# Forward DFT-47 as 24x24 products on sixteen 32x32 parts, with near and far frequencies formed on GpSimd

## The chip, the cores and the metric

The kernel runs on one core of a Trainium2 chip. The metric is the device time of one execution in microseconds (us). An execution is one launch over all inputs; the times below are those of whole executions, and the profile is that of one of them. Engines are named as in the profile: PE is TensorE's matmul, PEld its weight load, DVE is VectorE, ACT ScalarE, POOL GpSimd, and SP issues DMAs.

## What is computed

The reference is a Fourier layer along the sequence and an expert layer behind it (8 batches, 3008 positions, 256 channels, 2048 hidden units):

```python
X = np.fft.rfft(x, axis=1)
Yr = Xr @ w_r - Xi @ w_i + b_r
Yi = Xr @ w_i + Xi @ w_r + b_i
Yr = np.sign(Yr) * np.maximum(np.abs(Yr) - 0.01, 0.0)   # Yi alike
y = np.fft.irfft(Yr + 1j * Yi, n=3008, axis=1)
h = y.reshape(24064, 256) @ moe_w_in
out = (h * np.cos(h)) @ moe_w_out
```

## The kernel before

3008 is 64 x 47, two coprime lengths, so the transform of a batch is a DFT of length 64 and one of length 47 with an index order that needs no twiddle factors. The mixing matrices and the soft threshold (`wmix`) lie between the forward and the inverse transform. Each batch's Fourier work goes in these stages, by generator functions inside `tile_body`:

- `stage_a` (tiles `pa`, `ao`) does the forward DFT-64 and writes `scr1` in DRAM.
- `stage_b.load`, `forward` and `combine` do the forward DFT-47 for a quarter `q` of the 32 slots (eight slots). `load` brings the rows of `scr1` into `at`, and the constant `fq`. `forward` is one burst of 16 matmuls of 48x64 (`pb<-at,fq`): two groups `g` of 48 input rows (24 each of two symmetry parts or of real and imaginary part), an output block of 64 that holds the two halves `z` of 32, near and far frequency. Four banks `pb` receive it. DVE transposes each bank by 32x32 blocks into `at` again, and two DMAs by way of DRAM (`scrF`) turn it into `z`, where channels lie on partitions.
- `combine` (L598) makes of `z` the three operands of the mixing by matrices in split precision: real part, imaginary part and their sum `both`, each as a rounded value `Xh` (ACT) and a remainder `Xl`. POOL adds `both` (L610) and takes the remainders of `both` and of the imaginary part (`rest_pool`, L331), DVE those of the real part (`rest`, L334).
- `wmix` (tiles `pw`, L676 to L678) multiplies and thresholds; its `fold` (POOL, L706 to L718) turns signs by the table `sgn` and makes sums and differences for the inverse; `spread` does the inverse DFT-47 on sixteen 24x32 parts (`pi<-y,iw`) and writes `scr2`; `stage_c` (`pc`) does the inverse DFT-64 and gives `xTh`, `xTl`.

`moe_step` and `second` are the expert layer: for each of six tiles of up to 512 positions of a batch and each of 16 blocks `f` of hidden units six matmuls `ph` (L936 to L938), five elementwise passes on ACT and DVE with a cast `gh` and a remainder `gl`, and three steps later six matmuls `po` (L918 to L922). The remainder `gl` is taken by POOL for even `f` (L331) and by DVE for odd `f` (L334). Such a pair of `ph` and `po` groups is called a step here; there are 768.

Batch 0's Fourier work stands by itself ahead of everything and uses other code (`f2t1`). That of batch b + 1 is mixed into the expert steps of batch b: each generator yields a cost, and `pull` takes pieces as long as a budget lasts that each step adds to. The sum of these costs is written out by hand in `COST`; dividing it by the steps sets how densely the pieces are pulled. The instruction order of each engine then comes out of a scheduler that reorders within what is free to move, held by `floor()`, which ties a piece to the products of the second last step. A burst's matmuls are kept together:

```python
ins = mm(*calls[0][0], **calls[0][1])          # L373
...
with tc.high_priority(), tc.issue_after(ins.ins):
    for a, k in calls[1:]:
        ins = mm(*a, **k)                      # L383
```

So the first matmul of every burst has line L373 and the others have L383. In the trace a float32 matmul has two records, one for each of its two passes.

Of the kernel before, what the change touches and what calls it, by code (L numbers as in the profile page):

```python
# [88 lines left out]
def _constants():  # L89
# [17 lines left out]
    f1 = f1.transpose(0, 1, 3, 4, 2).reshape(128, 128)  # L107
    ei = ei.reshape(128, 128)
    fa = np.concatenate([fa.reshape(64, 64)] * 2)
# [4 lines left out]
    order = np.concatenate([np.arange(24), np.arange(46, 23, -1), [47]])  # L114
    f2 = np.zeros((32, 2, 48, 2, 48))
# [54 lines left out]
    c_fq = fq.transpose(1, 2, 0, 3, 4).reshape(128, 32 * 64).astype(np.float32)  # L170
    c_sig = np.concatenate([np.ones((48, 32)), sig.T]).astype(np.float32)
# [4 lines left out]
    c_sgn = c_sgn.astype(np.uint16)  # L176
    return [np.ascontiguousarray(a) for a in (c_fq, c_sig, c_f3, c_ff, c_if, c_iw, c_sgn)]


@with_exitstack  # L180
def tile_body(ctx: ExitStack, tc, x, w_r, w_i, b_r, b_i, w_in, w_out,
              c_fq, c_sig, c_f3, c_ff, c_if, c_iw, c_sgn, out):
    nc = tc.nc
# [355 lines left out]
    def stage_b(b):  # L539
# [15 lines left out]
        def load(q):  # L555
            if b and q < 4:
                fq = wk.tile([128, 512], F32, tag="fq", name="fq", bufs=2)
                with tc.issue_after(mark["x0"].ins) if b == 1 else ExitStack():
                    loads = [nc.gpsimd.dma_start(fq, c_fq[:, 512 * q:512 * q + 512])]
                t = wk.tile([128, 2048], F32, tag="at", name="at", bufs=1)  # L560
                for h in range(4):
                    own = q == 0 and SLOT0[h] != SLOTS[h]
                    r0 = 64 * (h // 2) + 24 * (h % 2)
# [10 lines left out]
        def forward(q):  # L574

            t, fq, loads = at.pop(q)
            p = some("pb", 4)
            burst(4, [((p[2 * e + g][64 * v:64 * v + 64, 256 * j:256 * j + 256],
                        fq[64 * g:64 * g + 48, 64 * i:64 * i + 64], t[64 * g:64 * g + 48, 256 * i:256 * i + 256]),
                       dict(start=j == 0, stop=j == 1, skip_group_check=True))  # L580
                      for e in range(2) for j in range(2) for v in range(2) for g in range(2) for i in (4 * v + 2 * e + j,)], loads)
            turned = t.rearrange("p (a g c e s k) -> p e g s c a k", a=4, g=2, c=2, e=2, s=2)
            for e in range(2):
                for g in range(2):
                    pv = p[2 * e + g]
                    drained(pv, nc.vector.transpose(turned[:, e, g], pv.rearrange("p (s c a k) -> p s c a k", s=2, c=2, a=4)))
                    if e == 0 or g == 0:
                        yield Hold(READ)
            f = dr.tile([128, 2048], F32, tag="scrF", name=f"scrF_{b}_{q}")
# [8 lines left out]
        def combine(q):  # L598

            z = Z.pop(q).rearrange("p (v z g m k) -> p g v z m k", v=2, z=2, g=2, m=8)[..., :24]  # L600
            xyh = wk.tile([128, 2304], F32R, tag="Xh", name="Xh", bufs=1)
            xyl = wk.tile([128, 2304], F32R, tag="Xl", name="Xl", bufs=1)
            hi, lo = ([m[:, 768 * r:768 * r + 768].rearrange("p (v m z k) -> p v z m k", v=2, m=8, z=2) for r in range(3)]
                      for m in (xyh, xyl))
            X[q] = tuple([[m[:, 768 * r:768 * r + 768].rearrange("p (v c x) -> p c v x", v=2, c=2)[:, c] for c in range(2)]
                          for r in range(3)] for m in (xyh, xyl))
            both = wk.tile([128, 1024], F32, tag="wx", name="both", bufs=3)[:, :768].rearrange("p (v m z k) -> p v z m k", v=2, m=8, z=2)
            for v in range(2):
                with floor():
                    nc.gpsimd.tensor_tensor(out=both[:, v], in0=z[:, 0, v], in1=z[:, 1, v], op=ALU.add)  # L610
                yield 0.9
                with floor():
                    nc.scalar.copy(hi[2][:, v], both[:, v])  # L613
                yield 0.8
            for v in range(2):
                with floor():
                    rest_pool(lo[2][:, v], both[:, v], hi[2][:, v])
                    nc.scalar.copy(hi[0][:, v], z[:, 0, v])
                yield 0.9
                with floor():  # L620
                    rest(lo[0][:, v], z[:, 0, v], hi[0][:, v])
                yield 0.9
            for v in range(2):
                with floor():
                    nc.scalar.copy(hi[1][:, v], z[:, 1, v])
                yield 0.8
                with floor():
                    rest_pool(lo[1][:, v], z[:, 1, v], hi[1][:, v])
                yield 1.2
# [70 lines left out]
        def fold(q, e):  # L700
# [14 lines left out]
            for r in range(2):  # L715
                po.tensor_tensor(out=od[:, 1 - r, first:, :23], in0=st[:, e, first:, r, 1:24],  # L716
                                 in1=st[:, e, first:, r, 24:47], op=ALU.subtract)
            po.tensor_tensor(out=st[:, e, first:, :, 1:24], in0=st[:, e, first:, :, 1:24],  # L718
                             in1=st[:, e, first:, :, 24:47], op=ALU.add)
            yield TURN  # L720
# [410 lines left out]
```

## Time and profile before

| | |
|---|---|
| median of 3 runs | 2578.68 us (2576.16 to 2579.6) |
| the profiled execution, its own time | 2579.13 us |
| span of the profile, first to last instruction | 2577.1 us |
| TensorE clock granted, mean | 0.998 |
| HBM traffic over the span | 109 GB/s |

The span is 2.0 us shorter than the execution's own time, which has the start and the end around it. A share is busy time over the span. In the timeline a row gives start and length, in us, of instructions of one line merged in order of time, their count, and in brackets idle time of the engine before it with what ended it. Busy time of PE is that of overlapping matmuls, so a stretch of it is measured from the start of one matmul to the start of a later one.

### The profile page before, as it was taken

To read this page: it belongs to the slowest core of one execution; us is meant where nothing else is said; L and a number is where in the kernel's file an instruction comes from. 1 tells how busy PE (TensorE), PEld (TensorE's weight loads), DVE (VectorE), ACT (ScalarE), POOL (GpSimd) and SP (SyncE) were. 2 spreads that over 40 slices of the span, in tenths; PEclk is the share of its full clock that TensorE was granted. 3 is DMA by queue.
4 is the path that set the end of the run, shared out by engine and by line. 5 is a ranking of instruction groups with operands and counts; after the bars stand their busy time and mean duration, and the time that the engine had idled before them with its cause. 6 is when DMAs were issued, how large, how long until landed. Compare 5 with 4: busy or idle time off the path is not lost.

```text
span 2577.1 us, 42991 instructions
## 1 busy us (share of the span) xinstructions
PE 2549.1 (99%) x15961; PEld 2063.7 (80%) x15961; DVE 1850.8 (72%) x2909; ACT 1679.6 (65%) x3119; POOL 1026.6 (40%) x1002
## 2 busy tenths in 40 slices
PE   9999999999999999999999999999999999999999
PEld 7577777877788777887788777887788888888888
DVE  5887766777667776777767777677776777766665
ACT  5766666666666666666666666666676666666666
POOL 2135552555334453345623545245442444222222
PEclk9999999999999999999999999999999999999999
DMA  7545444444334443254423544345433244210000
GB/s 238 188 115 148 134 116 118 112 130 139 111 82 126 136 132 98 82 154 142 130 83 98 155 131 119 91 101 144 132 104 104 85 116 114 62 45 17 17 25 16
DMA packets 172954, 283.12 MB, mean 110 GB/s; under 512 B 15608, under 2 KB 114200, under 8 KB 169160
## 3 DMA queue, kind: packets, MB, share of 16 engines
q1 hardware_dynamic: 161896, 243.78, 33.6%
q0 software_dynamic: 10112, 35.53, 4.4%
q8 instruction: 126, 2.06, 0.3%
q10 hardware_dynamic: 736, 1.05, 0.1%
q14 instruction: 84, 0.69, 0.1%
HBM read 149.76 MB, written 130.55 MB: 109 GB/s over the span
## 4 chain that ended last, share of the span: by engine, by line
PE 85%; DVE 5%; DMA 3%; ACT 2%; issue 2%; POOL 2%; SPq 0%; ACTq 0%; DVEq 0%; POOLq 0%
PE ph L936 12%; PE po L918 12%; PE po L922 12%; PE ph L937 12%; PE ph L938 12%; PE po L919 12%; PE pw L676 2%; PE pw L678 2%; PE pw L677 2%; PE pc L383 1%; PE pb L383 1%; DVE u L950 1%; DMA xt<-in_dram 1%; DVE u L947 1%; PE pw L672 1%
## 5 line engine op out<-in xcount | busy, mean ns | idle before, releaser
L331 POOL TENSOR_TENSOR gl<-u,gh 128x512 fp32r<-128x512 f32 (+1 forms) x384 | 494.0, 1286 | 1079.9 <-ACT gh L951 913.9
L949 ACT ACTIVATE u<-u 128x512 f32<-128x512 f32 (+1 forms) x768 | 478.4, 623 | 348.0 <-DVE u L947 346.9
L947 DVE SCALAR_TENSOR_TENSOR u<-ph,u 128x512 f32<-128x512 f32 (+1 forms) x768 | 515.9, 673 | 258.4 <-ACT u L946 256.5
L950 DVE TENSOR_TENSOR u<-ph,u 128x512 f32<-128x512 f32 (+1 forms) x768 | 518.5, 676 | 252.7 <-ACT u L949 240.5
L946 ACT ACTIVATE u<-ph 128x512 int32<-128x512 f32 (+1 forms) x768 | 449.9, 587 | 256.1 <-PE ph L938 248.0
L918 PE MATMUL po<-gh,wout 128*128 128x512 f32 (+1 forms) x1536 | 598.9, 390 | 4.4 <-ACT gh L951 4.4
L936 PE MATMUL ph<-xTh,win 128*128 128x512 f32 (+1 forms) x1536 | 601.5, 392 | 0.2
L951 ACT CAST gh<-u 128x512 fp32r<-128x512 f32 (+1 forms) x768 | 467.6, 610 | 202.3 <-DVE u L950 198.3
L937 PE MATMUL ph<-xTl,win 128*128 128x512 f32 (+1 forms) x1536 | 594.5, 387 | 0.0
L938 PE MATMUL ph<-xTh,win 128*128 128x512 f32 (+1 forms) x1536 | 594.0, 387 | 0.0
L919 PE MATMUL po<-gh,wout 128*128 128x512 f32 (+1 forms) x1536 | 593.6, 386 | 0.0
L922 PE MATMUL po<-gl,wout 128*128 128x512 f32 (+1 forms) x1536 | 477.8, 388 | 5.2 <-POOL gl L331 5.2
L334 DVE TENSOR_TENSOR gl<-u,gh 128x512 fp32r<-128x512 f32 (+1 forms) x384 | 304.6, 793 | 76.1 <-ACT gh L951 68.1
L936 PEld LDWEIGHTS ph<-xTh,win 128*128 128x128 f32 x1536 | 288.5, 188 | 87.5 <-issue 19.0
L922 PEld LDWEIGHTS po<-gl,wout 128*128 128x128 f32 x1536 | 287.2, 188 | 71.9 <-POOL gl L331 9.6
L918 PEld LDWEIGHTS po<-gh,wout 128*128 128x128 f32 x1536 | 288.6, 188 | 66.1 <-ACT gh L951 7.6
L938 PEld LDWEIGHTS ph<-xTh,win 128*128 128x128 f32 x1536 | 288.8, 188 | 56.3
L919 PEld LDWEIGHTS po<-gh,wout 128*128 128x128 f32 x1536 | 288.8, 188 | 51.1 <-issue 0.4
L937 PEld LDWEIGHTS ph<-xTl,win 128*128 128x128 f32 x1536 | 288.8, 188 | 51.0
L676 PE MATMUL pw<-Xh,wf 128*128 128x384 f32 x336 | 114.3, 340 | 2.9 <-ACT Xh L613 2.9
L716 POOL TENSOR_TENSOR odd<-st 128x184 f32<-128x184 f32 (+1 forms) x112 | 66.7, 595 | 122.0 <-DVE st L693 119.4
L677 PE MATMUL pw<-Xh,wf 128*128 128x384 f32 x336 | 113.4, 338 | 0.0
(119 smaller groups left out, 2443.6 us busy)
## 6 DMA issues: line engine op xcount, KB each, us to landing
scrF<-at SPq DMA_DIRECT2D x28, 1024.0 KB
z<-scrF SPq DMA_DIRECT2D x112, 256.0 KB
scrT<-tr SPq DMA_DIRECT2D x56, 512.0 KB
y<-scrT SPq DMA_DIRECT2D x112, 256.0 KB
bt<-scr SPq DMA_DIRECT2D x94, 256.0 KB
scr<-bo SPq DMA_DIRECT2D x224, 96.0 KB
scr<-ao SPq DMA_DIRECT2D x80, 256.0 KB
out_dram<-ob SPq DMA_DIRECT2D x80, 256.0 KB
```

Of the source, the lines that this page charges most:

```text
L331: return nc.gpsimd.tensor_tensor(out=lo, in0=x, in1=hi.bitcast(F32), op=ALU.subtract)
L918: mm(po[e][:, :n], wo[0][:, 0, f, es], gh[:, :n], start=f == 0, stop=False)
L919: mm(po[e][:, :n], wo[0][:, 1, f, es], gh[:, :n], start=False, stop=False)
L922: mm(po[e][:, :n], wo[0][:, 0, f, es], gl[:, :n], start=False, stop=f == NFC - 1)
L936: mm(h, win[:, 0, c, fs], th[:, c, :n], start=c == 0, stop=False)
L937: mm(h, win[:, 0, c, fs], tl[:, c, :n], start=False, stop=False)
L938: ins = mm(h, win[:, 1, c, fs], th[:, c, :n], start=False, stop=c == 1)
L946: nc.scalar.activation(k[:, :n], h, AF.Identity, bias=0.25, scale=1.0 / TWO_PI)
L947: nc.vector.scalar_tensor_tensor(out=u[:, :n], in0=h, scalar=1.0 / TWO_PI, in1=k[:, :n], op0=ALU.mult, op1=ALU.subtract)
L949: nc.scalar.activation(u[:, :n], u[:, :n], AF.Sin, bias=HALF_PI, scale=TWO_PI)
L950: product = nc.vector.tensor_tensor(out=u[:, :n], in0=h, in1=u[:, :n], op=ALU.mult)
L951: step = [nc.scalar.copy(gh[:, :n], u[:, :n])]
```

## The change

The forward burst of batches 1 to 7 is cut into 32 matmuls of 24x32 in place of 16 of 48x64: one for each of four row groups `h` of 24 input rows (at partitions 0, 32, 64 and 96), and each of the eight slots. A row group no longer adds over the two symmetry parts inside the matmul, and near and far frequency are no longer two outputs; instead `z` holds the two parts apart. `combine` makes near as their sum and far as their difference, for the real part (`re`) and the imaginary part (`im`), and multiplies the far half of `im` by a table `far` of signs: five more POOL instructions per quarter. Real and imaginary part then lie in whole runs, and everything behind works on halves of 384 elements that are contiguous. The order of the 48 output frequencies changes so that the empty one stands first in the far half; the fold reads 25 to 47 in place of 24 to 46. `fq` is half as large, slot 0 is kept in another form, and `COST` has 15.5 in place of 11.0 for the new yields.

```diff
-    fq = np.zeros((32, 2, 64, 2, 32))
+    fq = np.zeros((32, 2, 2, 32, 32))
...
-                fq[sl, g, 24 * o:24 * o + 24, :, :24] = parts[v, sl, r, :, g]
+                fq[sl, g, o, :24, :24] = parts[v, sl, r if sl else 0, :, g, 0]
...
+    far = sig[:, :24] * sig[:, 24:]
+    far[0] *= -1
...
+    turn_far = cp.tile([128, 32, 24], BF16, name="far")
...
+        nc.gpsimd.dma_start(turn_far.rearrange("p s k -> p (s k)"), c_far.bitcast(BF16))
...
             p = some("pb", 4)
-            burst(4, [((p[2 * e + g][64 * v:64 * v + 64, 256 * j:256 * j + 256],
-                        fq[64 * g:64 * g + 48, 64 * i:64 * i + 64], t[64 * g:64 * g + 48, 256 * i:256 * i + 256]),
-                       dict(start=j == 0, stop=j == 1, skip_group_check=True))
-                      for e in range(2) for j in range(2) for v in range(2) for g in range(2) for i in (4 * v + 2 * e + j,)], loads)
...
+            burst(4, [((p[h][64 * v + 32 * j:64 * v + 32 * j + 32, 256 * e:256 * e + 256],
+                        fq[32 * h:32 * h + 24, 32 * i:32 * i + 32], t[32 * h:32 * h + 24, 256 * i:256 * i + 256]),
+                       dict(start=e == 0, stop=e == 1, skip_group_check=True))
+                      for e in range(2) for v in range(2) for j in range(2) for h in range(4) for i in (4 * e + 2 * v + j,)], loads)
...
+            part = [wk.tile([128, 1024], F32, tag="wx", name=n, bufs=3)[:, :768] for n in ("re", "im", "both")]
+            both = part[2]
+            with_far = turn_far[:, 8 * q:8 * q + 8].unsqueeze(1).to_broadcast([128, 2, 8, 24])
+            for r in range(2):
+                for n, op in enumerate((ALU.add, ALU.subtract)):
+                    to = part[r].rearrange("p (m w z k) -> p z w m k", m=4, w=4, z=2)[:, n]
+                    with floor():
+                        nc.gpsimd.tensor_tensor(out=to, in0=z[:, 2 * r], in1=z[:, 2 * r + 1], op=op)
+                    yield 0.9
+            with floor():
+                far = part[1].rearrange("p (c y z k) -> p z c y k", c=2, y=8, z=2)[:, 1]
+                nc.gpsimd.tensor_tensor(out=far, in0=far, in1=with_far, op=ALU.mult)
+            yield 0.9
...
-                    nc.gpsimd.tensor_tensor(out=both[:, v], in0=z[:, 0, v], in1=z[:, 1, v], op=ALU.add)
+                    nc.gpsimd.tensor_tensor(out=cut(both, v), in0=cut(part[0], v), in1=cut(part[1], v), op=ALU.add)
...
-    COST = 4 * (6 * GROUP + 2 * TURN + 11.0 + MIXED + QUIET + 3 * READ + BURST + QUIET + 3 * READ + BURST)
+    COST = 4 * (6 * GROUP + 2 * TURN + 15.5 + MIXED + QUIET + 3 * READ + BURST + QUIET + 3 * READ + BURST)
```

The change also moves instructions on every engine, since the scheduler orders them anew. Two places are shown. The first is PE's order at the last quarter's forward burst of batch 3 (`po`, `ph`: expert layer; `pb`: the burst), before:

```order
L918 MATMUL po_8994<-gh,wout 128x512
L919 MATMUL po_8994<-gh,wout 128x512
L373 MATMUL pb<-at,fq 64x256
L383 MATMUL pb<-at,fq 64x256 x15
L936 MATMUL ph<-xTh,win 128x512
L937 MATMUL ph<-xTl,win 128x512
```

and now:

```order
L944 MATMUL po_9243<-gl,wout 128x512
L944 MATMUL po_9244<-gl,wout 128x512
L380 MATMUL pb<-at,fq 32x256
L390 MATMUL pb<-at,fq 32x256 x31
L958 MATMUL ph<-xTh,win 128x512
L959 MATMUL ph<-xTl,win 128x512
```

The burst stands at the same step, between whole groups of `po` and `ph`, and has twice as many matmuls with half as many output rows each. The second place is POOL's order at the combination of the last quarter of batch 3 (`gl`: expert layer; `st<-st`: the fold's sum), before:

```order
L331 TENSOR_TENSOR gl<-u,gh 128x512
L610 TENSOR_TENSOR both<-z 128x2x8x24 x2
L718 TENSOR_TENSOR st<-st 128x16x23
L331 TENSOR_TENSOR Xl<-both,Xh 128x2x8x24 x2
L331 TENSOR_TENSOR gl<-u,gh 128x512
L331 TENSOR_TENSOR Xl<-z,Xh 128x2x8x24 x2
```

and now:

```order
L338 TENSOR_TENSOR gl<-u,gh 128x512
L617 TENSOR_TENSOR re<-z 128x4x4x24 x2
L617 TENSOR_TENSOR im<-z 128x4x4x24 x2
L740 TENSOR_TENSOR st<-st 128x16x23
L338 TENSOR_TENSOR gl<-u,gh 128x512
L621 TENSOR_TENSOR im<-im,far 128x16x24
L632 TENSOR_TENSOR both<-re,im 128x384 x2
L338 TENSOR_TENSOR Xl<-im,Xh 128x384 x2
L338 TENSOR_TENSOR gl<-u,gh 128x512
L338 TENSOR_TENSOR Xl<-both,Xh 128x384 x2
```

The four sums and the fold's sum stand between two remainders `gl`, and the remainders of `im` now go ahead of those of `both`.

## Rows read from the trace of the kernel before

**Rows 1.** The page, busy us of each engine, share of the span, instructions:
```profile
PE 2549.1 (99%) x15961; PEld 2063.7 (80%) x15961; DVE 1850.8 (72%) x2909; ACT 1679.6 (65%) x3119; POOL 1026.6 (40%) x1002
```
**Rows 2.** Waits of PEld; waiter and awaited, us in total, times, longest us:
```profile
PEld po L922 <- POOL gl L331: 9.6, 12, 2.2
```
**Rows 3.** Timeline, PE, a forward burst; start us, length us, engine, instruction, count:
```profile
1039.28 0.43 PE L373 MATMUL pb<-at,fq 48*64 48x256 f32 x1
...
1039.56 1.69 PE L383 MATMUL pb<-at,fq 48*64 48x256 f32 x27
1041.17 0.47 PE L936 MATMUL ph<-xTh,win 128*128 128x448 f32 x1
```
**Rows 4.** Groups by line and form, PE; busy us, mean ns of one, idle before:
```profile
L383 PE MATMUL pb<-at,fq 48*64 48x256 f32 x840 | 54.6, 381 | 0.0
```
**Rows 5.** Timeline, PE, an inverse burst:
```profile
1004.80 0.61 PE L373 MATMUL pi<-y,iw 24*32 24x512 f32 x1
1004.80 0.70 PE L383 MATMUL pi<-y,iw 24*32 24x512 f32 x15
...
1005.26 0.68 PE L383 MATMUL pi<-y,iw 24*32 24x512 f32 x15
1005.87 0.50 PE L936 MATMUL ph<-xTh,win 128*128 128x512 f32 x1
```
**Rows 6.** Groups by line and form, POOL:
```profile
L331 POOL TENSOR_TENSOR gl<-u,gh 128x512 fp32r<-128x512 f32 x320 | 419.7, 1312 | 843.6 <-ACT gh L951 733.6 <-issue 72.4 <-PE po L922 24.4
...
L331 POOL TENSOR_TENSOR Xl<-both,Xh 128x384 fp32r<-128x384 f32 x56 | 69.4, 1252 | 3.7 <-ACT Xh L613 3.2 <-PE ph L938 0.5
L610 POOL TENSOR_TENSOR both<-z 128x384 f32<-128x384 f32 x56 | 59.6, 1076 | 3.1 <-DMA z<-scrF 3.1
L706 POOL TENSOR_TENSOR st<-st,sgn 128x384 f32<-128x384 f32 x56 | 55.6, 993 | 63.0 <-DVE st L693 57.5 <-PE ph L938 5.5
```
**Rows 7.** Timeline, POOL, the last combination of batch 3:
```profile
935.23 2.00 POOL L610 TENSOR_TENSOR both<-z 128x384 f32<-128x384 f32 x2
937.17 1.00 POOL L718 TENSOR_TENSOR st<-st 128x368 f32<-128x368 f32 x1
938.11 2.77 POOL L331 TENSOR_TENSOR Xl<-both,Xh 128x384 fp32r<-128x384 f32 x2
940.85 1.61 POOL L331 TENSOR_TENSOR gl<-u,gh 128x512 fp32r<-128x512 f32 x1
942.42 2.42 POOL L331 TENSOR_TENSOR Xl<-z,Xh 128x384 fp32r<-128x384 f32 x2
```
**Rows 8.** Timeline, PE, where the mix of that combination's last part begins:
```profile
945.72 0.39 PE L938 MATMUL ph<-xTh,win 128*128 128x512 f32 x1
945.95 0.33 PE L676 MATMUL pw<-Xh,wf 128*128 128x384 f32 x1
```
**Rows 9.** Groups by line and form, DVE, the whole run, then 2300 to 2560 us:
```profile
L334 DVE TENSOR_TENSOR gl<-u,gh 128x512 fp32r<-128x512 f32 x320 | 263.4, 823 | 69.3 <-ACT gh L951 61.3 <-PE ph L938 0.7 <-PE po L922 0.7
...
L334 DVE TENSOR_TENSOR gl<-u,gh 128x512 fp32r<-128x512 f32 x40 | 27.6, 691 | 3.8 <-ACT gh L951 3.8
```
**Rows 10.** Timeline, POOL and PE, a late `gl`; then busy time, clock in a window:
```profile
651.21 1.29 POOL L460 TENSOR_TENSOR xe<-xt 128x512 f32<-128x512 f32 x1 [3.52 <-DMA xt<-in_dram]
...
657.97 1.26 POOL L331 TENSOR_TENSOR gl<-u,gh 128x512 fp32r<-128x512 f32 x1
...
657.12 0.39 PE L919 MATMUL po<-gh,wout 128*128 128x512 f32 x1
659.28 0.73 PE L922 MATMUL po<-gl,wout 128*128 128x512 f32 x2 [1.77 <-POOL gl L331]
...
660.50:663.70 3.20, 3.20 (x9) 2.51 (x9) 2.27 (x4) 0.82 (x2) 0.52 (x1) 0.52 0.52 127
```

More of the change, by code (lines that the diff above doesn't have):

```diff
@@ L108, in _constants @@
     ei = ei.reshape(128, 128)
+    fa[:, 0, 0], fa[:, 0, 1] = (1 + alt) / 2, (1 - alt) / 2
     fa = np.concatenate([fa.reshape(64, 64)] * 2)
@@ L113, in _constants @@
     C, S = np.cos(th), np.sin(th)
-    order = np.concatenate([np.arange(24), np.arange(46, 23, -1), [47]])
+    order = np.concatenate([np.arange(24), [47], np.arange(46, 23, -1)])
     f2 = np.zeros((32, 2, 48, 2, 48))
@@ L176, in _constants @@
     c_sgn = c_sgn.astype(np.uint16)
-    return [np.ascontiguousarray(a) for a in (c_fq, c_sig, c_f3, c_ff, c_if, c_iw, c_sgn)]
+    return [np.ascontiguousarray(a) for a in (c_fq, c_sig, c_f3, c_ff, c_if, c_iw, c_sgn, c_far)]
 @with_exitstack
 def tile_body(ctx: ExitStack, tc, x, w_r, w_i, b_r, b_i, w_in, w_out,
-              c_fq, c_sig, c_f3, c_ff, c_if, c_iw, c_sgn, out):
+              c_fq, c_sig, c_f3, c_ff, c_if, c_iw, c_sgn, c_far, out):
     nc = tc.nc
@@ L556, in load @@
             if b and q < 4:
-                fq = wk.tile([128, 512], F32, tag="fq", name="fq", bufs=2)
+                fq = wk.tile([128, 256], F32, tag="fq", name="fq", bufs=2)
                 with tc.issue_after(mark["x0"].ins) if b == 1 else ExitStack():
-                    loads = [nc.gpsimd.dma_start(fq, c_fq[:, 512 * q:512 * q + 512])]
+                    loads = [nc.gpsimd.dma_start(fq, c_fq[:, 256 * q:256 * q + 256])]
                 t = wk.tile([128, 2048], F32, tag="at", name="at", bufs=1)
@@ L577, in forward @@
             p = some("pb", 4)
[L578 to L588 removed]
+            burst(4, [((p[h][64 * v + 32 * j:64 * v + 32 * j + 32, 256 * e:256 * e + 256],
+                        fq[32 * h:32 * h + 24, 32 * i:32 * i + 32], t[32 * h:32 * h + 24, 256 * i:256 * i + 256]),
+                       dict(start=e == 0, stop=e == 1, skip_group_check=True))
+                      for e in range(2) for v in range(2) for j in range(2) for h in range(4) for i in (4 * e + 2 * v + j,)], loads)
+            turned = t.rearrange("p (a h c e k) -> p h e c a k", a=4, h=4, c=2, e=2)
+            for h in range(4):
+                drained(p[h], nc.vector.transpose(turned[:, h], p[h].rearrange("p (e c a k) -> p e c a k", e=2, c=2, a=4)))
+                if h < 3:
+                    yield Hold(READ)
             f = dr.tile([128, 2048], F32, tag="scrF", name=f"scrF_{b}_{q}")
@@ L598, in combine @@
         def combine(q):
-            z = Z.pop(q).rearrange("p (v z g m k) -> p g v z m k", v=2, z=2, g=2, m=8)[..., :24]
+            z = Z.pop(q).rearrange("p (w h m k) -> p h w m k", w=4, h=4, m=4)[..., :24]
             xyh = wk.tile([128, 2304], F32R, tag="Xh", name="Xh", bufs=1)
             xyl = wk.tile([128, 2304], F32R, tag="Xl", name="Xl", bufs=1)
-            hi, lo = ([m[:, 768 * r:768 * r + 768].rearrange("p (v m z k) -> p v z m k", v=2, m=8, z=2) for r in range(3)]
-                      for m in (xyh, xyl))
@@ L605, in combine @@
-            X[q] = tuple([[m[:, 768 * r:768 * r + 768].rearrange("p (v c x) -> p c v x", v=2, c=2)[:, c] for c in range(2)]
+            X[q] = tuple([[m[:, 768 * r + 384 * c:768 * r + 384 * c + 384] for c in range(2)]
                           for r in range(3)] for m in (xyh, xyl))
-            both = wk.tile([128, 1024], F32, tag="wx", name="both", bufs=3)[:, :768].rearrange("p (v m z k) -> p v z m k", v=2, m=8, z=2)
+            part = [wk.tile([128, 1024], F32, tag="wx", name=n, bufs=3)[:, :768] for n in ("re", "im", "both")]
@@ L608, in combine, with half, cut @@
+            yield 0.9
+            def half(m, r, v):
+                return m[:, 768 * r + 384 * v:768 * r + 384 * v + 384]
+            def cut(m, v):
+                return m[:, 384 * v:384 * v + 384]
             for v in range(2):
                 with floor():
-                    nc.gpsimd.tensor_tensor(out=both[:, v], in0=z[:, 0, v], in1=z[:, 1, v], op=ALU.add)
+                    nc.gpsimd.tensor_tensor(out=cut(both, v), in0=cut(part[0], v), in1=cut(part[1], v), op=ALU.add)
                 yield 0.9
@@ L612, in combine @@
                 with floor():
-                    nc.scalar.copy(hi[2][:, v], both[:, v])
+                    nc.scalar.copy(half(xyh, 2, v), cut(both, v))
                 yield 0.8
@@ L616, in combine @@
                 with floor():
-                    rest_pool(lo[2][:, v], both[:, v], hi[2][:, v])
-                    nc.scalar.copy(hi[0][:, v], z[:, 0, v])
+                    rest_pool(half(xyl, 2, v), cut(both, v), half(xyh, 2, v))
+                    nc.scalar.copy(half(xyh, 0, v), cut(part[0], v))
                 yield 0.9
                 with floor():
-                    rest(lo[0][:, v], z[:, 0, v], hi[0][:, v])
+                    rest(half(xyl, 0, v), cut(part[0], v), half(xyh, 0, v))
                 yield 0.9
@@ L624, in combine @@
                 with floor():
-                    nc.scalar.copy(hi[1][:, v], z[:, 1, v])
+                    nc.scalar.copy(half(xyh, 1, v), cut(part[1], v))
                 yield 0.8
                 with floor():
-                    rest_pool(lo[1][:, v], z[:, 1, v], hi[1][:, v])
+                    rest_pool(half(xyl, 1, v), cut(part[1], v), half(xyh, 1, v))
                 yield 1.2
@@ L716, in fold @@
                 po.tensor_tensor(out=od[:, 1 - r, first:, :23], in0=st[:, e, first:, r, 1:24],
-                                 in1=st[:, e, first:, r, 24:47], op=ALU.subtract)
+                                 in1=st[:, e, first:, r, 25:48], op=ALU.subtract)
             po.tensor_tensor(out=st[:, e, first:, :, 1:24], in0=st[:, e, first:, :, 1:24],
-                             in1=st[:, e, first:, :, 24:47], op=ALU.add)
+                             in1=st[:, e, first:, :, 25:48], op=ALU.add)
             yield TURN
```

6 lines of the change are left out of this document (4 added, 2 removed).

## Prediction

> **What bounds the kernel now.** I read the page first, then the waits of TensorE, then single stretches of the timeline. The page says that PE is busy for 99% of the span, DVE for 72% and POOL for 40% [rows 1]. Busy time alone could be padding, since matmuls overlap, so the waits count: in the whole run TensorE's weight loads waited for POOL's `gl` only 12 times, 9.6 us together [rows 2]. PE is therefore a queue with hardly a hole in it. A microsecond of PE time that goes is a microsecond of the run, as long as no other engine comes to stand in its place; POOL is the one that gets more to do.
>
> **The forward burst on PE.** Look at one burst of `pb` in the timeline [rows 3]. Its first matmul starts at 1039.28 and the next `ph` matmul at 1041.17: 1.89 us. The 16 matmuls of 48x64 run as 32 records (840 of them at L383 are 30 in each of 28 bursts [rows 4], two more are at L373), four side by side, so eight rounds of 256 columns. Now look at the inverse burst `pi` [rows 5]: 16 matmuls on sixteen 24x32 parts, two rounds of 512 columns, and the next `ph` starts 1005.87 - 1004.80 = 1.07 us after the first. The changed forward burst has 32 matmuls of 24x32, that is 64 records, sixteen side by side: four rounds of 256 columns, the same columns per part as in `pi`. So `pi` is the nearest row. Two more changes of round than in `pi` cost a little (the fifteen later parts of a round start over 0.70 - 0.61 = 0.09 us [rows 5], most of it under the running round); I take 1.09 us. The bounds are 1.07, as `pi`, and 1.89, no gain at all. What it costs to enter and to leave the small parts is in neither span, and is taken to stay. Saved: 0.80 us x 28 = **22.4 us**.
>
> The Trainium skill speaks against this (TensorE: Matmul & The Clock Gate, Part 3): a pack of tiles takes one matmul's duration plus some 4 ns for each further tile, as if packs stood one behind another. In the row the 27 last records, nearly seven rounds, take 1.69 us together where a single record takes 0.43 [rows 3], so rounds do overlap; by that model the burst would save almost nothing (rival 2).
>
> **What PE, DVE, ACT and the queues get besides.** The four transposes of a burst keep shape and count and stand one behind another in DVE's order as before; their banks are now full together at the end of a burst that ends earlier: 0. ACT makes six casts per combination, as before: 0. The `fq` loads stay 28 in number, with half the bytes, behind the same waits on POOL: 0. One constant more (`far`) is loaded at the start on POOL's queue, ahead of the later `raw` loads, of which several stand ready before they are split: 0, bounds 0 and 1 us, one of POOL's operations [rows 6]. The new constant order only moves which 23 columns the fold reads: 0. `COST` grows with the new yields, so the pieces of Fourier work are pulled a little denser and end where they ended: 0. `re`, `im` and `both` now use all three `wx` buffers; their readers are done long before the next combination: 0.
>
> **POOL.** Each of 28 combinations gets four sums and one product. A sum of this form is `both` today, 1076 ns; a product with a table is the sign product of the fold, 993 ns [rows 6]. That is 28 x (4 x 1.076 + 0.993) = 148 us more on POOL, 1027 [rows 1] to 1175 us, 46% of the span. Against it stands that `both` and the remainders `Xl` now read and write whole runs of 384 instead of pieces of 24; the row of `Xl` has a mean of 1252 ns for 384 elements while `gl`, in whole runs, takes 1312 for 512 [rows 6], so up to 0.27 us may go from each of 112 remainders; bounds 0 and -30 us. None of this is on the path by itself. What matters is whether something that PE reads comes late, and that is looked for in the tightest of a batch's four combinations, the last (q = 3).
>
> There, before, POOL runs `both` from 935.23, the fold's sum, two `Xl`, a `gl` and two more `Xl` up to 942.42 + 2.42 = 944.84 [rows 7], and PE's mix of that part begins at 945.95 [rows 8]: 1.1 us to spare. In the new order (second place of the order above) two `re`, two `im` and the fold's sum stand ahead of the first `gl`, then the product, two `both`, two `Xl`, a `gl` and two `Xl`. With the durations of [rows 6, 7] (1.0 a sum here, 1.0 the fold's, 1.3 a `gl`, 1.0 the product, 1.0 to 1.3 an `Xl`, its bounds) that is 935.2 + 4.0 + 1.0 + 1.3 + 1.0 + 2.0 + 2.0 to 2.6 + 1.3 + 2.0 to 2.6 = 949.8 to 951.0, 5.0 to 6.2 us later. PE's order gives way too: counting `ph` rows, the first `pw` of this mix stands behind 247 steps before and 248 now, and a step is twelve matmuls of 0.23 us (945.72 to 945.95 [rows 8]), 2.8 us. Slack and step make 3.9 us, so 1.1 to 2.3 us are left over. From that goes what PE's order moves the single `Xl` matmuls further back, three to six `ph` matmuls, 0.7 to 1.4 us. I take 0.7 us for this combination, between the bounds 0 and 2.3, and nothing for the other three, whose mixes stand further behind the combination in PE's order: 7 x 0.7 = **4.9 us** of new waiting.
>
> **DVE** shares something with POOL: `gl` on DVE takes 823 ns over the run but 691 ns in the last stretch [rows 9], where nothing but its own `gl` is left to POOL. So the 320 large `gl` lose 42 us to POOL already, and with 14% more POOL work they lose some 6 us more, in pieces of a few hundred ns on an engine with 28% idle: 0 in the sum.
> The Trainium skill (GPSIMD Engine Reference, 8. Key points) says that POOL shares its SBUF interfaces with VectorE and that instructions with two SBUF inputs suffer; these rows agree. Were DVE on the path, the sum would lose those 6 us.
>
> **Sum.** The profiled execution took 2579.13 us (span 2577.1). 2579.1 - 22.4 + 4.9 = 2561.6; the median of the runs is 0.45 lower, so 2561.2, said as **2561 us**.
>
> **Rivals.**
> 1. *Half of it goes into waits for POOL.* If each of the 28 combinations leaves PE waiting for 0.4 to 0.6 us, 11 to 17 us go: 2567 to 2573. For it: five more operations stand ahead of `both` everywhere. Against it: the queue was reordered with them in it.
> 2. *The burst does not shorten.* If each round of sixteen waits out the one before at the spacing seen in `pi` (0.45 us from 1004.80 to 1005.26 [rows 5]), the burst takes 3 x 0.45 + 0.09 + 0.31 = 1.75 us and saves 0.14 x 28 = 4 us; with the waits that is 2580, no change. That is what the skill's model of packs would give. Against it: in `pi` the spacing is that of 512 columns, twice as many.
> 3. *Slower: POOL late, then a slow clock.* It has happened: four sums of an `xt` fold and a sign product ran from 651.21 on, `gl` began only at 657.97, and PE, whose last matmul began at 657.12, went on at 659.28, 1.9 us lost. Then the granted clock was 0.52 from 660.5 to 663.7, the lower of its levels (1.2 of 2.4 GHz), another 1.5 us [rows 10]. Price 3.4 us. It decides from seven such events on (22.4 / 3.4 = 6.6). Two in each of the seven batches cost 48 us: 2604. Against it: the new run of operations ahead of a `gl`, 5.0 us here, is shorter than the 6.8 us that did it there.
>
> **Chances.** Forecast 0.72, reaching from 2553 (no new waits, 2556, and some old ones gone) to 2567; rival 1 0.13; rival 2 0.06; rival 3 0.07; faster than 2553 0.02. A measurement of this kernel tells some 0.2%, 5.2 us, from no change. Faster: 0.72 + 0.12 + 0.02 = 0.86; same: 0.07, rival 2 and the end of rival 1; slower: 0.07. The range 2553 to 2573 holds the forecast and rival 1.
>
> **What would show it.** Right: the `pb` rows are 24x32 parts, 64 records a burst, and the next `ph` starts about 1.1 us after the first; POOL is busy for 1140 to 1175 us; PE's waits for `gl` stay under 20 us. Wrong: a burst of 1.7 us or more (rival 2); PE waiting for `gl` or `Xh`/`Xl` beside each combination (rival 1); stretches with a granted clock near 0.5 behind such waits (rival 3).

## The result: slower, and the profile after

The changed kernel takes **2604.47 us** (median of 4 runs, 2603.11 to 2608.08) against 2577.42 us of the kernel before on the same chip: a ratio of 1.0107, 95% interval 1.009 to 1.0125. It is 27 us slower. The forecast was 2561 with a range of 2553 to 2573. The profiled execution took 2603.11 us, its span is 2601.3.

The page of the changed kernel, busy us of each engine (before: [rows 1]):
```profile
PE 2547.9 (98%) x16857; PEld 2055.1 (79%) x16857; DVE 1865.0 (72%) x2909; ACT 1681.3 (65%) x3119; POOL 1175.0 (45%) x1143
```
POOL has the 1175 us that were worked out. PE is as busy as before, though its bursts are shorter: this row does not show holes well, since a matmul behind a wait is drawn longer (0.50 us in a row further down, for 0.39). The waits say more; here are PEld's and then PE's (waiter and awaited, us in total, times, longest; before: [rows 2]):
```profile
PEld po L940 <- ACT gh L973: 26.1, 26, 1.8
PEld po L944 <- POOL gl L338: 19.1, 21, 3.7
...
PE pa L380 <- DVE u L972: 6.7, 4, 1.7
```
and the same wait for `gh` before:
```profile
PEld po L918 <- ACT gh L951: 7.6, 9, 1.8
```
The waits for POOL's `gl` have doubled, from 9.6 to 19.1 us, just under the 20 that the forecast had set as its limit, but the larger share is for ACT's `gh`, which POOL does not make (26.1 us, 7.6 before), and a burst `pa` now waits for DVE's `u`.

The burst of PE in the timeline (before: [rows 3]; `pi`, which the forecast took as its model: [rows 5]):
```profile
1053.04 0.40 PE L380 MATMUL pb<-at,fq 24*32 24x256 f32 x1
1053.05 0.49 PE L390 MATMUL pb<-at,fq 24*32 24x256 f32 x15
1053.28 0.37 PE L380 MATMUL pb<-at,fq 24*32 24x256 f32 x1
1053.29 1.25 PE L390 MATMUL pb<-at,fq 24*32 24x256 f32 x47
1054.46 0.47 PE L958 MATMUL ph<-xTh,win 128*128 128x448 f32 x1
```
There are 64 records, and the next `ph` starts 1054.46 - 1053.04 = **1.42 us** after the first, not 1.09. Before it was 1.89.

POOL's groups (busy us, mean ns; before: [rows 6]) and then the `gl` of DVE (before: [rows 9]):
```profile
L617 POOL TENSOR_TENSOR im<-z 128x384 f32<-128x384 f32 x56 | 66.9, 1214 | 0.0
L338 POOL TENSOR_TENSOR Xl<-both,Xh 128x384 fp32r<-128x384 f32 x56 | 66.9, 1204 | 2.6 <-PE ph L960 2.1 <-ACT Xh L635 0.5
...
L621 POOL TENSOR_TENSOR im<-im,far 128x384 f32<-128x384 f32 x28 | 27.4, 978 | 0.6
```
```profile
L341 DVE TENSOR_TENSOR gl<-u,gh 128x512 fp32r<-128x512 f32 x320 | 288.7, 902 | 68.1 <-ACT gh L973 64.8
```
The new operations last what their neighbours did. DVE's `gl` went from 823 to 902 ns.

**Where the time went.** For every two consecutive large matmuls of PE (`ph`, `po`, `pw`) I took the time from start to start less the usual spacing of that width (0.227 us at 512 columns, 0.204 at 448, 0.171 at 384), and added these up by what lies between them, without the start of the run, where batch 0's Fourier work stands by itself. The columns are the largest changes, not all parts of the sum. All in us:

| kernel | bursts `pb` | bursts `pa` | `po` to `po` | `ph` to `po` | all of PE's losses |
|---|---|---|---|---|---|
| before | 56.5 | 35.7 | 17.9 | 2.7 | 237.1 |
| changed | 42.5 | 45.7 | 32.1 | 11.7 | 260.5 |
| without sums, paced | 43.1 | 36.1 | 15.5 | 4.3 | 222.7 |
| without sums, unpaced | 43.0 | 35.7 | 16.0 | 2.1 | 217.8 |
| with sums, unpaced | 42.4 | 36.4 | 36.3 | 2.2 | 248.6 |

The bursts `pb` gave 14 us. The sum still grew by 23, so new holes took 37. The last three rows are experiments.

### The profile page after: what moved, and what is told of

It is laid out like the page before. It is cut to its first block, busy times and chain, and to the rows that moved or that the text cites. A ratio compares the mean times of both kernels' runs of the same rounds, so it can differ in the third digit from the quotient of the medians.

```text
span 2601.3 us, 44758 instructions
## 1 busy us (share of the span) xinstructions
PE 2547.9 (98%) x16857; PEld 2055.1 (79%) x16857; DVE 1865.0 (72%) x2909; ACT 1681.3 (65%) x3119; POOL 1175.0 (45%) x1143
## 4 chain that ended last, share of the span: by engine, by line
PE 66%; DVE 11%; ACT 6%; DMA 6%; POOL 5%; issue 5%; SPq 0%; ACTq 0%; DVEq 0%; POOLq 0%
PE ph L958 10%; PE po L940 9%; PE ph L959 9%; PE ph L960 9%; PE po L944 9%; PE po L941 9%; DVE u L972 3%; DVE u L969 2%; ACT gh L973 2%; DVE gl L341 2%; ACT u L971 2%; DMA xt<-in_dram 2%; PE pw L698 1%; PE pw L699 1%; PE pw L700 1%
## 5 line engine op out<-in xcount | busy, mean ns | idle before, releaser
L972 DVE TENSOR_TENSOR u<-ph,u 128x512 f32<-128x512 f32 (+1 forms) x768 | 517.7, 676 | 252.7 <-ACT u L971 240.3
L341 DVE TENSOR_TENSOR gl<-u,gh 128x512 fp32r<-128x512 f32 (+1 forms) x384 | 329.3, 858 | 74.9 <-ACT gh L973 70.8
L940 PEld LDWEIGHTS po<-gh,wout 128*128 128x128 f32 x1536 | 288.5, 188 | 83.2 <-ACT gh L973 26.1
L944 PEld LDWEIGHTS po<-gl,wout 128*128 128x128 f32 x1536 | 286.0, 188 | 72.2 <-POOL gl L338 19.1
L960 PEld LDWEIGHTS ph<-xTh,win 128*128 128x128 f32 x1536 | 289.2, 188 | 56.5
L941 PEld LDWEIGHTS po<-gh,wout 128*128 128x128 f32 x1536 | 288.7, 188 | 51.1 <-issue 0.4
L698 PE MATMUL pw<-Xh,wf 128*128 128x384 f32 x336 | 113.6, 338 | 2.0 <-ACT Xh L635 2.0
L700 PE MATMUL pw<-Xl,wf 128*128 128x384 f32 x336 | 113.9, 340 | 0.3 <-POOL Xl L338 0.3
```

Source lines behind the costliest of these rows:

```text
L940: mm(po[e][:, :n], wo[0][:, 0, f, es], gh[:, :n], start=f == 0, stop=False)
L941: mm(po[e][:, :n], wo[0][:, 1, f, es], gh[:, :n], start=False, stop=False)
L944: mm(po[e][:, :n], wo[0][:, 0, f, es], gl[:, :n], start=False, stop=f == NFC - 1)
L960: ins = mm(h, win[:, 1, c, fs], th[:, c, :n], start=False, stop=c == 1)
L972: product = nc.vector.tensor_tensor(out=u[:, :n], in0=h, in1=u[:, :n], op=ALU.mult)
```

## The experiments

Every kernel was timed beside the kernel before on the same chip; the ratio is to that.

**1. Sums and pacing apart.** The change puts five operations into each combination and also five yields of 0.9, with `COST` grown by 4.5, by which the scheduler spaces the work. Four kernels cross the two:
```
  order alone        before:  + for _ in range(5): yield 0.9      COST 11.0 -> 15.5
  no sums, paced     changed: - sums, far product; re, im read from z; yields, COST 15.5 stay
  no sums, unpaced   the same: - yields                           COST 15.5 -> 11.0
  sums, unpaced      changed: - yields                            COST 15.5 -> 11.0
```
Order alone: 

> The kernel before, with five bare yields of 0.9 at the head of each combination and COST 15.5: no instruction is added, only the places at which the pieces of Fourier work stand between the expert steps move. Theory 1 (the five POOL operations themselves, late or in DVE's way, make the new waits): no change, 2574 to 2582 us. Theory 2 (the new waits come from the new placement and order): slower by a good part of the 38 us of new waits, 2600 us or more.

No sums, paced: 

> The changed kernel without its four sums and its product per combination (near and far frequencies are not formed; the operands of the mixing are taken from z as it lies), with the five yields and COST as they are. Theory 1: the waits go with the operations and the shorter burst's 13 us stay, about 2564 us (2560 to 2572). Theory 2: the waits stay, 2595 us or more.

No sums, unpaced: 

> As the one with no sums and paced (near and far frequencies are not formed), and without the five yields, COST 11.0: the shorter burst alone in about the old placement. Both theories: 2577 less 28 x 0.46 us = 2564 us (2560 to 2570). If it is above 2575, something else in the changed code waits, such as the larger burst's banks or the new order of the halves.

Sums, unpaced: 

> The changed kernel with its five POOL operations, but no yields for them and COST 11.0. Theory 1: no better than the changed kernel, 2600 us or more, since more POOL work is pulled into less time. Theory 2: near 2564 us plus little.

| | paced | unpaced |
|---|---|---|
| old burst | 2586.95, 1.0038 [1.0024, 1.0052] | 2577.43 (before) |
| new burst, no sums | 2566.51, 0.9963 [0.995, 0.9976] | 2560.13, 0.9937 [0.9922, 0.9952] |
| new burst, sums | 2604.47, 1.0107 [1.009, 1.0125] | 2588.78, 1.0045 [1.0029, 1.0061] |

The new burst without the sums gives 17 us (such a kernel leaves out the near and far frequencies). The sums cost 38 us with the pacing and 29 without. The pacing costs 6 to 16 us, 9.5 in the old kernel, where it brings no instruction at all. None of these terms was in the forecast at its size.

**2. The load alone, and the load on another engine.**
```
  load alone         before:  + 4 subtracts and 1 product of 128x384 on POOL per combination, into spare buffers
  sums on DVE        sums unpaced: nc.gpsimd -> nc.vector for the five
  sums split         the same for the two sums of re and the product
  remainders on DVE  sums unpaced: rest_pool -> rest for the four Xl that POOL makes
```
Load alone: 

> The kernel before, with its old burst and its old order costs, and with five more GpSimd operations at the head of each combination (four differences and one product of 128x384, written to two spare buffers that nobody reads). If the load on GpSimd alone is what costs (theory 1), it costs here what the sums cost in the changed kernel without pacing, 2588.8 - 2560.1 = 28.7 us, so 2577 + 20 to 35 = 2597 to 2612. If the cost of the sums needs the shorter burst (PE comes to each combination earlier) or that the combination itself waits for its sums (theory 2: what is late is the combination's own chain), it is under 12 us: 2577 to 2589.

Sums on DVE: 

> The changed kernel without the extra pacing, its four sums and the product on VectorE in place of GpSimd. If the cost is that GpSimd comes late with what stands behind the sums in its order (gl, the fold), it goes: VectorE gets 140 operations of 0.55 to 0.7 us, 80 to 100 us on an engine that is idle for a quarter; 2560 to 2570. If it is VectorE that is short (its operations get longer beside GpSimd, and the sums make its order longer still), the time stays at 2585 or grows to 2600.

Sums split: 

> As the run before, but only the sums of the real part and the product on VectorE; the two sums of the imaginary part stay on GpSimd. Theory 1 (GpSimd late): three of five operations gone from its order, so 28.7 x 2/5 = 11 us or less are left: 2562 to 2571. If VectorE is short: between 2575 and 2595.

Remainders on DVE: 

> The changed kernel without the extra pacing, all sums on GpSimd, but the four remainders that GpSimd makes in each combination on VectorE. GpSimd then has 28 operations more than in the kernel before instead of 140. If what counts is GpSimd's whole load, some 28.7/5 = 6 us are left: 2562 to 2570. If what counts is the row of sums that stands ahead of a gl at the head of a combination, it is still there, and the time stays at 2580 to 2590, or grows with what VectorE gets (112 operations of 0.55 to 1.2 us).

Measured: load alone 2608.52, 1.0132 [1.0116, 1.0149]; sums on DVE 2575.34, 0.9998 [0.9988, 1.0007]; split 2579.2, 1.0019 [1.0009, 1.0028]; remainders on DVE 2593.39, 1.0074 [1.0057, 1.009]. So five operations that nobody reads cost the old kernel 33 us: neither the shorter burst nor a reader of their results is needed for it. On DVE they cost 15 instead of 29. And to take four other operations from POOL while the sums stay gave nothing back. PE's waits in load alone:
```profile
PE pw L683 <- ACT Xh L620: 16.7, 10, 3.4
PE po L929 <- POOL gl L331: 12.9, 8, 4.0
```
There half of it shows as a late combination, whose `both` stands behind the five in POOL's order; in the changed kernel that wait is 2.0 us in all. The same load comes out at another wait.

**3. Is it the row of five?** In the run with the sums unpaced one place costs PE 2.7 to 3.0 us in five batches. POOL's timeline there, with PE's wait behind it:
```profile
1248.64 0.58 POOL L736 TENSOR_TENSOR odd<-st 128x184 f32<-128x184 f32 x1 [6.41 <-DVE st L713]
...
1249.35 1.30 POOL L338 TENSOR_TENSOR gl<-u,gh 128x512 fp32r<-128x512 f32 x1
1250.61 2.00 POOL L617 TENSOR_TENSOR re<-z 128x384 f32<-128x384 f32 x2
1252.55 2.44 POOL L617 TENSOR_TENSOR im<-z 128x384 f32<-128x384 f32 x2
1254.95 1.29 POOL L738 TENSOR_TENSOR st<-st 128x368 f32<-128x368 f32 x1
1256.19 1.22 POOL L620 TENSOR_TENSOR im<-im,far 128x384 f32<-128x384 f32 x1
1257.38 1.27 POOL L338 TENSOR_TENSOR gl<-u,gh 128x512 fp32r<-128x512 f32 x1
...
1258.70 0.50 PE L942 MATMUL po<-gl,wout 128*128 128x512 f32 x1 [2.86 <-POOL gl L338]
```
POOL idles for 6.4 us, and then four sums, the fold's sum and the product stand ahead of a `gl`. It looks as if the row only had to move into the idle time. Six runs tried that, all on top of the sums unpaced; in each the row of a batch's first combination stays where it was:
```
  early         the five ahead of the last product of the mix before (combinations 1 to 3, here and below)
  earlier       ahead of the inverse before that
  one by one    at five places of the mix, one each            (also on DVE)
  one by one, late   the same, behind the inverse burst        (also on DVE)
```
Early: 

> The changed kernel without the extra pacing, with the five GpSimd operations of a batch's combinations 1 to 3 issued one product (3.5 us of cost) and a fold earlier: ahead of the last product of the mix before, where GpSimd was seen idle for 6.4 us (1242.2 to 1248.6 in the run with the sums unpaced), in place of directly ahead of the fold's sum and a gl. The operations are the same in number and length, VectorE has the same neighbour. If what costs is the row of sums standing ahead of what others wait for, most of the 28.7 us goes: 2560 to 2570. If it is that VectorE's operations get longer beside GpSimd, wherever GpSimd runs, nothing goes: 2582 to 2592.

Earlier: 

> As the run before, but the five operations are issued another piece earlier, ahead of the inverse of the part before (GpSimd idle for 5.7 us there, 1235.3 to 1240.9, with a gl behind). By the row theory 2560 to 2572, near the run before; by the theory of the longer VectorE operations 2582 to 2592.

One by one: 

> The changed kernel without the extra pacing, with the five GpSimd operations of combinations 1 to 3 issued one at a time at five places of the mix before (about 6 us apart), instead of as a row. Moving the whole row gave 2585.5 and 2609.6, so a row of 5.5 us is in the way wherever it stands, if the reason is that a gl comes on GpSimd every 7 us or so and PE takes it at once. By that theory a single operation of 1.1 us mostly fits in: most of the 28.7 us goes, 2562 to 2572, with the rows of the seven combinations 0 left. If instead it is GpSimd's total work, or VectorE's operations that get longer beside it, the time stays between 2580 and 2592.

One by one on DVE: 

> As the run before, with the five operations on VectorE. As a row on VectorE they cost 2575.3 - 2560.1 = 15 us. If the row is what costs there too, 2560 to 2568; if it is VectorE's whole work, 2572 to 2580.

One by one, late: 

> As the run with the sums one at a time, but none of them before z has landed: they begin behind the inverse burst, one for each of its pieces, and what is not done by then stands at the head of the combination as before. By the theory of the row (whatever stands behind it in an engine's order comes late) 2563 to 2578; by that of GpSimd's whole work, or of VectorE's operations that get longer beside it, 2582 to 2592 as with the row in its place.

One by one, late, on DVE: 

> The same with the five operations on VectorE, where the row at the head of the combination cost 15 us (2575.3). By the theory of the row 2560 to 2570, faster than both kernels; by that of VectorE's whole work 2572 to 2580.

| | on POOL | on DVE |
|---|---|---|
| row, at the combination | 2588.78 | 2575.34 |
| early | 2585.51, 1.0036 [1.0023, 1.005] | |
| earlier | 2609.59, 1.0137 [1.012, 1.0153] | |
| one by one | 2622.64, 1.018 [1.0162, 1.0198] | 2653.21, 1.0299 [1.0284, 1.0315] |
| one by one, late | 2585.9, 1.0037 [1.0024, 1.0051] | 2595.67, 1.0073 [1.0061, 1.0086] |

The theory of the row falls. Moved early, or taken apart and late, the operations on POOL still cost 25 and 26 us, where the row costs 29, so the row itself is worth a few us at most; on DVE taking it apart makes 15 us into 35. "One by one" costs more still: the operations stand in their engine's order before `z` is there, and hold it up (in "earlier" this wait is only 16.3 us). POOL's waits in "one by one":
```profile
POOL im L616 <- DMA z<-scrF: 82.4, 15, 7.2
```

**4. More time for `gl` and `gh`.**
```
  SKEW 3 -> 4 (gh, gl: 5 buffers); both is written into z; wx: 3 -> 2 buffers; W_NEXT 13 -> 12
```
With sums: 

> The changed kernel without the extra pacing, its five operations on GpSimd in a row as they stand there, but PE uses gh and gl four steps after their ph and not three (SKEW 4, one more buffer of each; the room comes from both, which is written into z, and from one buffer less for the early weights). Every gh and gl gets one step, 2.7 us, more. If what costs is that gh and gl come late at PE by 1 to 3 us, behind the row on GpSimd or behind VectorE, most of the 28.7 us goes: 2560 to 2570. If PE loses the time in other waits (u behind VectorE, the combination itself) or all engines are simply slowed, it stays at 2578 to 2590.

Without: 

> The same for the kernel without the sums and the far product (these parts of the combination are left out): what the fourth step does by itself. Its gh and gl waits are some 8 us, of which part goes: 2552 to 2562. The difference between this run and the run before is the cost of the sums with the longer reach: under 10 us by the theory of late gh and gl, 20 to 30 us by the other.

With sums 2627.68, 1.0197 [1.0183, 1.0211]; without 2588.43, 1.0045 [1.0032, 1.0059]. PE's waits with sums:
```profile
PE po L939 <- ACT ob L947: 43.2, 11, 6.3
...
PE po L939 <- ACT gh L972: 2.7, 3, 1.3
PE po L943 <- POOL gl L338: 2.2, 2, 1.9
```
The waits for `gl` and `gh` are gone, as the theory of late `gl` had it, and the sums still cost 39 us: PE now waits for ACT's `ob` (4.4 us without the sums). The longer reach itself, with the smaller buffers that make room for it, costs 28 us. So the wait that shows a loss is not its cause; it is where PE next reads something that came late.

Behind such a wait a second loss can follow. PE in the same run (the last row is a stretch with its length, the busy time of PE, PEld, DVE, ACT and POOL, and the granted clock):
```profile
570.82 0.80 PE L939 MATMUL po<-gh,wout 128*128 128x512 f32 x1 [2.77 <-ACT ob L947]
...
570.80:576.90 6.10, 6.08 (x14) 4.81 (x15) 4.20 (x7) 5.27 (x11) 6.01 (x6) 0.50 0.31 101
```
The granted clock is 0.50, the lower of its levels (1.2 of 2.4 GHz), after PE has stood idle for 2.8 us, and in such a stretch large matmuls start 0.43 us apart in place of 0.23. Added up over all these stretches after the first 100 us, this costs 19.6 us here and 4.1 in the run without sums: 15 of the 39 us. It is 6.5 us with the sums unpaced and 1.6 without sums, 10.3 in load alone and 2.2 in the kernel before. So 5 to 8 us of what the load costs in those runs is a slower TensorE. These are sums from one trace each.

**5. The burst.**
```
  by rows   16 products of row groups 0, 1 (e = 0, then e = 1), then 16 of row groups 2, 3
  in two    burst(calls[:16]); yield Hold(READ); burst(calls[16:])
```
By rows: 

> The kernel without sums and pacing (it leaves out the sums and the far product, so it computes something else), with the 32 products of a burst in another order: first all 16 of two row groups (eight parts, then the same eight parts for the other half of the columns' sum), then all 16 of the other two. If the hole of 0.19 us and the wider spacing of 16.7 ns come with the 33rd record, as for a queue that holds so many instructions ready, they stay at the 33rd record. If they come with the second product into the same part, they come at the 17th. The whole burst (first pb to next ph) gets no shorter than 1.43 us either way.

In two: 

> The kernel without sums and pacing (the same parts left out), with each forward burst cut into two of 16 products (32 records), some five other matmuls apart. If only so many instructions stand ready ahead, each half has both rounds at 6.7 ns from part to part, no hole, and takes 0.24 + 0.10 us from its first to its last record. If the second products into a part are slow by themselves, the second half keeps the 16.7 ns. The time of the run: entering and leaving twice costs what the hole gave, 2555 to 2570.

By rows 2568.5 us, in two 2564.57, one run each, beside 2560.13 with the whole burst. The first half of a burst cut in two:
```profile
461.66 0.40 PE L380 MATMUL pb<-at,fq 24*32 24x256 f32 x1
...
461.90 0.37 PE L380 MATMUL pb<-at,fq 24*32 24x256 f32 x1
...
462.30 0.50 PE L949 MATMUL ph<-xTh,win 128*128 128x512 f32 x1
```
a burst by rows:
```profile
820.72 0.40 PE L380 MATMUL pb<-at,fq 24*32 24x256 f32 x1
...
822.44 0.50 PE L946 MATMUL ph<-xTh,win 128*128 128x512 f32 x1
```
and, in the changed kernel, a burst `pc` of the inverse DFT-64, four parts of 64x64 side by side:
```profile
1193.59 0.27 PE L380 MATMUL pc<-ff,bt 64*64 64x64 f32 x1
...
1193.71 1.05 PE L390 MATMUL pc<-ff,bt 64*64 64x64 f32 x59
```
Each half takes 0.64 us, 1.29 both together, and in both halves the records of a round start 6.7 ns apart. (21 of the 28 bursts are cut so; in the other seven the halves stood back to back and ran as one.) In the whole burst the first 32 records keep this pace too. The 33rd starts with its round, then comes a hole of 0.19 us, and the rest start 16.7 ns apart: 16 x 16.7 = 267 ns for sixteen parts, more than the 0.24 us from round to round before. By rows, eight second products into a part, from 0.46 us after the first record on, still start 7 ns apart, so it is not the second product that is slow. The wide spacing begins 0.65 us after the first record, as in the whole burst. The burst by rows takes 1.72 us, 0.30 more than the whole one, and 28 x 0.30 = 8 us is what that run is slower by.

So in this burst the pace changes behind some 32 records, or 64 instructions with the weight load that each record has. The Trainium skill (TensorE: Matmul & The Clock Gate, Part 3) gives TensorE a reorder window of 64 instructions; these rows fit that, and no run here varies the number itself. That the count alone does it is not shown: `pc` has 64 records too, each with a weight load, and the parts of its rounds start 6.7 ns apart to the last, a round of four every 58 ns.

## Why the prediction was wrong, step by step

- **"PE is a queue with hardly a hole"; a microsecond of PE is a microsecond of the run.** Right: without sums and pacing, the bursts lose 13.5 us less and other waits 6 less (237.1 to 217.8), and the run is 17 us shorter.
- **The burst, 22.4 us.** Right in kind, mis-sized: 1.42 us, inside the bounds 1.07 to 1.89 but not near `pi`. It saved (1.89 - 1.42) x 28 = 13 us. Rounds do overlap, they start 0.24 us apart, so rival 2 was wrong too; but `pi` has 32 records and is over where the slow pace begins. The row "nearest" in columns was not near in the number of instructions.
- **"COST … end where they ended: 0".** Wrong: 9.5 us in the old kernel, 16 with the sums. The three `wx` buffers, also put at 0, were right: over the whole run POOL is idle ahead of `re` for 2.9 us, for `z`, and for no buffer.
- **POOL's load.** Right: 148 us, 1175 in all. The 0.27 us per remainder hardly came (1252 to 1204 ns).
- **The tightest combination, 0.7 us x 7 = 4.9.** Near in size, by luck in part. PE loses 3.0 us there in batch 2, 0.87, 0.88 and 1.6 in batches 4 to 6, 6.4 in all, and nothing above 0.5 in batch 3, the one that was read. But only 2.0 us of it is the mix waiting for the combination; the rest is `po` waiting for a `gh` or `gl`.
- **"Nothing for the other three."** This is the step that failed. PE loses 1.52, 0.95 and 1.74 us at three other places of a batch, in four or five batches each: some 22 of the 37 us of new holes, 10 of them at `pa`. At the first and the third no sum is near (the second, a wait for `gh` some 10 us behind a combination's sums, was not followed). The chain at the first of the three, in the timeline of all engines, where no sum has run for 60 us and the next run from 1200.2 on:
```profile
1192.31 0.58 POOL L738 TENSOR_TENSOR odd<-st 128x184 f32<-128x184 f32 x1 [5.38 <-DVE st L715]
...
1192.92 0.45 DVE L746 STREAM_TRANSPOSE tr<-odd 128x256 f32<-128x256 f32 x1 [0.69 <-POOL odd L738]
...
1193.29 0.65 DVE L969 SCALAR_TENSOR_TENSOR u<-ph,u 128x512 f32<-128x512 f32 x1
...
1194.09 0.98 POOL L740 TENSOR_TENSOR st<-st 128x368 f32<-128x368 f32 x1
...
1195.11 0.77 DVE L745 STREAM_TRANSPOSE tr<-st 128x256 f32<-128x256 f32 x2 [1.16 <-POOL st L740]
...
1196.49 0.63 ACT L971 ACTIVATE u<-u 128x512 f32<-128x512 f32 x1 [1.88 <-DVE u L969]
...
1198.16 0.50 PE L940 MATMUL po<-gh,wout 128*128 128x512 f32 x1 [1.34 <-ACT gh L973]
```
DVE stands before `tr<-st` until POOL's `st` is done, the `u` behind it come late, then ACT's `gh`, then PE. In the kernel without sums but paced, the same three operations of POOL follow one another at the same distances (1.78 us from `odd` to `st` in both), and DVE does two more `u` operations first:
```profile
1170.82 0.58 POOL L729 TENSOR_TENSOR odd<-st 128x184 f32<-128x184 f32 x1 [5.38 <-DVE st L706]
...
1171.43 0.45 DVE L737 STREAM_TRANSPOSE tr<-odd 128x256 f32<-128x256 f32 x1 [0.69 <-POOL odd L729]
1171.80 1.25 DVE L960 SCALAR_TENSOR_TENSOR u<-ph,u 128x512 f32<-128x512 f32 x2
...
1172.60 0.99 POOL L731 TENSOR_TENSOR st<-st 128x368 f32<-128x368 f32 x1
...
1173.15 0.69 DVE L963 TENSOR_TENSOR u<-ph,u 128x512 f32<-128x512 f32 x1
1173.76 0.76 DVE L736 STREAM_TRANSPOSE tr<-st 128x256 f32<-128x256 f32 x2
```
  No wait, no loss. So at that place it is not POOL that works longer: the added instructions have changed the order of DVE where none of them had run for 60 us. That the scheduler orders anew was before my eyes in the listings; I looked at the places around the sums alone.
- **DVE beside POOL, 6 us and 0 in the sum.** Mis-sized: its large `gl` lost 288.7 - 263.4 = 25 us, though DVE's busy time as a whole grew by only 14 (1850.8 to 1865.0). How much of that reaches PE was not measured. A place where it does is the third of the three, in the timeline:
```profile
1233.71 1.28 POOL L338 TENSOR_TENSOR gl<-u,gh 128x512 fp32r<-128x512 f32 x1 [7.03 <-ACT gh L973]
...
1234.09 1.32 DVE L715 SCALAR_TENSOR_TENSOR st<-cl,st 128x384 f32<-128x384 f32 x1 [0.59 <-ACT cl L714]
...
1237.46 0.64 PE L380 MATMUL pa<-xt,ff 64*64 64x512 f32 x1 [1.68 <-DVE u L972]
```
  DVE's `st` takes 0.55 us when it is alone; here it ends 0.42 us after POOL's `gl`, the `u` behind it are late, and `pa` waits. The Trainium skill (SBUF — State Buffer, SBUF: two separate sides) says that the shared pair of ports is locked for a whole instruction and the other side blocks; this row agrees.
- **Rival 3, 2604 us.** Its number is that of the result by luck; its mechanism has a small part in it. It happens in full at the first combination of batch 1, one of the three that were given nothing. POOL and PE in the timeline:
```profile
160.68 1.98 POOL L617 TENSOR_TENSOR re<-z 128x384 f32<-128x384 f32 x2 [2.95 <-DMA z<-scrF]
162.61 2.42 POOL L617 TENSOR_TENSOR im<-z 128x384 f32<-128x384 f32 x2
164.99 1.26 POOL L338 TENSOR_TENSOR gl<-u,gh 128x512 fp32r<-128x512 f32 x1
...
166.31 1.22 PE L944 MATMUL po<-gl,wout 128*128 128x512 f32 x2 [3.26 <-POOL gl L338]
167.32 0.63 PE L958 MATMUL ph<-xTh,win 128*128 128x512 f32 x1
167.75 0.63 PE L959 MATMUL ph<-xTl,win 128*128 128x512 f32 x1
```
  PE waits 3.3 us for the `gl` behind the four sums, and the granted clock is 0.50 behind that, the matmuls 0.43 us apart: some 5 us in all. But in the whole run after the first 100 us the half clock costs the large matmuls 4.6 us against 2.2 before, and a `pa` at 601.8 another 1.7; the mean granted clock is 0.996, against 0.998 before. The other losses are many of 1 to 2 us, not two of 3.4 per batch with a slow clock behind.

**What stays open.** The five operations cost 25 us or more on POOL at every place where they were tried. It is shown that a reader of their results and the shorter burst are not needed for it, and that neither the row nor a late `gl` alone is the reason. Two causes remain, and no run parts them: that each operation holds up DVE, on POOL by blocking its operations with two operands in SBUF, on DVE by its own time (15 us there), and that each version of the program gets another order on every engine. The half clock behind long waits adds to either. A kernel with the sums and an order held fixed was not tried. No version that computes the reference beat the kernel before: the best, with the sums on DVE, is level with it.

## What to carry to other kernels

Where one engine is full and all others feed it in fixed order, an added operation on a half idle engine is not free: here 140 operations of 1.1 us on POOL cost at least 25 us, some 0.2 us each, wherever they stood. Before it is costed at nothing, compare the order of every engine in the whole period, not only around the edit, and measure the scheduling numbers alone. And when a row is taken as the price of another burst, match the number of instructions too, not only the columns.

## What the hardware showed that was not expected

The burst of 24x32 matmuls runs at 6.7 ns from part to part for its first 32 records, then at 16.7 ns with a hole of 0.19 us ahead. Two halves of 32 take 1.29 us against 1.42 to 1.43 whole, but entering and leaving twice uses that up: the bursts' share of PE's losses is the same within 0.1 us, and the one run (2564.57 us) was not faster than the whole burst (2560.13). And DVE's operations on two SBUF operands get longer beside one of POOL: in the changed kernel `st` (L715) takes 0.55 us alone and 0.93 in the mean where POOL runs at the same time (1.32 in the row above), while those with an operand in PSUM, like `u` (L972, 512 columns), keep their mean of 686 ns, before and now.
